# A planner's rule for operations on one PSUM tile: dependence on every earlier operation of the other engines instead of the latest of each, with a new table of due-time offsets

## The chip, the cores and the metric

The kernel runs on one core of one Trainium2 chip. The metric is device time in microseconds, the median of three runs. One execution was also profiled; rows quoted below come from that one.

## What is computed

Pooled attention followed by a feed-forward layer with a rational activation, 4608 tokens (8 x 576), model width 512 (8 heads of 64), hidden width 2048:

```python
k_p = k.reshape(B, H, S // 8, 8, D).mean(axis=3)      # same for v
scores = q @ k_p.T / sqrt(D)
attn = softmax(scores)
x = (attn @ v_p) as (B*S, H*D)
h = x @ w_in
P = a[0] + a[1]*h + a[2]*h*h + a[3]*h*h*h
Q = 1 + abs(b[0])*abs(h) + abs(b[1])*h*h
out = (P / (Q + 1e-6)) @ w_out
```

The weights arrive in 64-bit floats; the kernel decodes each into a high and a low 32-bit part, and splits activations the same way, so that each large product is three products (high x high, low x high, high x low).

## The kernel before

The 4608 tokens are 18 blocks of 256 (`i`), the hidden width is 8 units of 256 (`u`): 144 units (i, u), listed in `order` (lines 942 to 945). For a block, `attend` (line 787) prepares pooled keys and values, makes scores, softmax and the attention output `x` (tiles `qT`, `ps`, `mx`, `e`, `sm`, `am`, `pv`, `x`). For a unit, `mm1` (line 837) makes `ph` = h in a PSUM bank with 24 matmuls on TensorE, `rational` and `quotient` (lines 850 and 866) turn it into `gh` and `gl`, and `mm2` (line 887) adds their products with `wout` into two PSUM banks `po` with 24 matmul halves. After a block's last unit the `po` are evicted and stored.

The quotient of one unit is a chain over three engines. ScalarE (ACT) makes `w` = |h| (line 867), `t` = a3 h + a2 (line 868) and `r` = b1 w + b0 (line 869). GpSimd (POOL) multiplies `w` by `r` (line 870). VectorE (DVE) makes `t` times h (line 871) and then (t + a1) times h (line 872). ACT takes the reciprocal of the denominator as Ln and Exp into the PSUM tile `rp` (lines 874, 875); DVE joins the two sides in three steps (lines 876 to 881); ACT copies the high part `gh` (line 882), POOL makes the low part `gl` (line 883). Lines 867, 868, 871 and 872 all read the PSUM tile `ph`. `w`, `t` and `r` lie in a ring of seven buffers (`rat`, line 381); the operation `w` claims all three tiles of its unit (`claims=early`), the operation `t` only its own.

None of this is issued in the order of the text. Each operation is handed to `Plan.add` (line 146) with an engine, a cost and a due time. `add` collects dependencies: by data, and for tiles in PSUM (`ring.tag == "ps"`, lines 169 to 173) on operations of other engines. Due times come from `due(at)` (line 948) with `HEAD`, `PACE`, `SLOW` (line 946); the second half of a unit is due five units later (`LAG`). `solve` (line 189) carries due times backwards along the dependencies, adds the hand-made or searched offsets of the table `LATER` (by operation number, line 115), and then fills the engines greedily: on each engine the operation that can start first, and among those within 0.02 us of it the one due first (lines 237 to 239). `issue` (line 283) emits the operations in the order found. Each engine then executes its own list strictly in that order, and the framework puts the semaphores: an operation on a PSUM tile waits for what other engines were issued on that tile before it, reads included.

Line 315 issues every planned operation, so every row of the profile carries L315, and groups are told apart by tile names; line 307 issues filler matmuls at the start (`idle`).

Of the kernel before, what the change touches and what calls it, by code (L numbers as in the profile page):

```python
# [22 lines left out]
class Lazy:  # L23


    def __init__(self, tile, chain=()):
        self.tile, self.chain = tile, chain
# [41 lines left out]
def meet(a, b):  # L69
    return all(x0 < y1 and y0 < x1 for (x0, x1), (y0, y1) in zip(a, b))  # L70


class Buf:


    def __init__(self, ring, shape, dtype, name):
        self.ring, self.shape, self.dtype, self.name = ring, shape, dtype, name
        self.writes, self.reads, self.left, self.held, self.it = [], [], 0, False, None
        self.slot, self.latest = None, {}

    def real(self):
        if self.it is None:
# [18 lines left out]
class Plan:  # L101
# [11 lines left out]


    LATER = {
# [15 lines left out]
    }  # L131
    HOLD = {}

# [12 lines left out]
    def add(self, eng, cost, calls, port=False, claims=(), bytes=0, early=34.0, after=()):  # L146
        op = Op()
        op.eng, op.cost, op.port, op.calls, op.bytes = eng, cost, port, calls, bytes
        op.early, op.slack, op.lead = early, self.slack, 0.0
        op.seq, op.due, op.deps, op.users = len(self.ops), self.now, set(), []  # L150
        touched = {}
        for _, args, kw in calls:
            every = list(args) + list(kw.values())
            dst = kw.get("out", args[0] if args else None)
            for v in every:
                if isinstance(v, Lazy) and v is not dst:
                    box = v.box()
                    op.deps.update(o for o, x in v.tile.writes if meet(x, box))
                    v.tile.reads.append((op, box))
                    touched[id(v.tile)] = v.tile  # L160
            if isinstance(dst, Lazy):
                t, box = dst.tile, dst.box()
                op.deps.update(o for o, x in t.writes if meet(x, box))
                op.deps.update(o for o, x in t.reads if meet(x, box))
                if box == ():
                    t.writes, t.reads = [], [r for r in t.reads if r[0] is op]
                t.writes.append((op, box))
                touched[id(t)] = t
        for t in touched.values():
            if t.ring.tag == "ps":  # L170

                op.deps.update(o for e, o in t.latest.items() if e != eng)
                t.latest[eng] = op
        op.deps.update(after)
        op.deps.discard(op)
        for c in claims:
            touched[id(c.tile)] = c.tile
        op.bufs = list(touched.values())
        for b in op.bufs:
            b.left += 1  # L180
        self.ops.append(op)
        return op
# [151 lines left out]
def tile_pooled_attention_then_rational_moe(  # L334
# [32 lines left out]
    NA = NU // 2  # L367
# [575 lines left out]
    order += [(i, u) for u0 in (0, NA) for i in (2, 3) for u in range(u0, u0 + NA)]  # L943
    order += [(i, u) for i in range(2) for u in range(NA, NU)]
    order += [(i, u) for i in range(4, NBLK) for u in range(NU)]
    HEAD, PACE, SLOW, SLOWS = 15.0, 5.5, 4.5, 2 * NA

    def due(at):
        return HEAD + SLOW * min(at, SLOWS) + PACE * max(0, at - SLOWS)
# [78 lines left out]
```

## Time and profile before

| | |
|---|---|
| median of 3 runs | 913.93 us (913.83 to 915.69) |
| the profiled execution | 912.12 us |
| its span | 910.2 us |
| TensorE busy | 887.5 us, 98% |
| VectorE busy | 761.2 us, 84% |
| ScalarE busy | 675.0 us, 74% |
| GpSimd busy | 526.1 us, 58% |

The span is the time from the first to the last instruction of the profiled execution; 1.9 us of that execution lie outside it. PE is TensorE's matmuls, PEld its weight loads, which run ahead of the matmuls. "Idle before" and the brackets at the end of a timeline row say how long the engine had nothing to do before that instruction, and which instruction ended it.

### The profile page before, as it was taken

What the parts mean: (1) busy time and instruction counts of PE and PEld (TensorE: products, weight loads), DVE (VectorE), ACT (ScalarE), POOL (GpSimd) and SP (SyncE); (2) the same over time, 40 slices, a digit from 0 to 9 for tenths busy, and PEclk for the clock granted to TensorE, in tenths of its full rate; (3) what the DMA queues carried; (4) which work ended last, traced back from release to release, by engine and by line L of the source; (5) the groups of instructions that cost most, each with busy time, mean ns of one, the idle gap of its engine ahead of it and who ended that gap; (6) DMA issues with size and microseconds to landing.
All of it is one profiled execution on the core that took longest, in us unless ns stands there. A gap on an engine that the chain in (4) does not pass through costs nothing.

```text
span 910.2 us, 17165 instructions
## 1 busy us (share of the span) xinstructions
PE 887.5 (98%) x6132; PEld 823.3 (90%) x6132; DVE 761.2 (84%) x1337; ACT 675.0 (74%) x1124; POOL 526.1 (58%) x472
## 2 busy tenths in 40 slices
PE   8899999999999999999999999999999999999998
PEld 7898899899998999999999899989888999999997
DVE  7899888879889899959997888798979899578874
ACT  4799879859487868658886675785849697577874
POOL 5776867876357545446745743546635754435554
PEclk9999999999999999999999999999999999999999
DMA  9994201154144312122603341323322411202000
GB/s 294 344 393 150 53 24 47 47 149 96 43 91 115 84 31 57 30 54 60 138 10 72 93 88 35 48 50 99 79 45 59 93 45 31 52 1 35 25 24 23
DMA packets 185081, 75.31 MB, mean 83 GB/s; under 512 B 162341, under 2 KB 162341, under 8 KB 184997
## 3 DMA queue, kind: packets, MB, share of 16 engines
q1 hardware_dynamic: 184996, 74.23, 31.3%
q8 instruction: 48, 0.79, 0.4%
q14 instruction: 37, 0.29, 0.1%
HBM read 50.59 MB, written 12.58 MB: 69 GB/s over the span
## 4 chain that ended last, share of the span: by engine, by line
PE 55%; ACT 18%; DVE 12%; SPq 5%; issue 4%; DMA 4%; POOL 2%; ACTq 0%; POOLq 0%; DVEq 0%
PE ph L315 25%; PE po L315 22%; DVE t L315 6%; SPq L315 5%; ACT rp L315 4%; ACT r L315 3%; ACT t L315 3%; ACT w L315 3%; PE ps L315 3%; PE pv L315 2%; ACT gh L315 2%; DMA q<-in_q_dram 2%; DVE rp L315 1%; ACT am L315 1%; DMA st_v<-in_v_dram 1%
## 5 line engine op out<-in xcount | busy, mean ns | idle before, releaser
L315 PEld LDWEIGHTS ph<-x,win 128*128 128x128 f32 x3264 | 436.4, 191 | 28.1 <-DVE t L315 1.0
L315 PE MATMUL ph<-x,win 128*128 128x256 f32 x3264 | 447.5, 276 | 2.2 <-DVE t L315 0.9
L315 PE MATMUL po<-wout,gh 128*128 128x512 f32 x1152 | 325.6, 383 | 2.6 <-ACT gh L315 1.4
L315 POOL TENSOR_TENSOR w<-w,r 128x512 f32<-128x512 f32 (+1 forms) x145 | 190.9, 1317 | 213.1 <-ACT r L315 197.1
L315 POOL TENSOR_TENSOR gl<-t,gh 128x512 fp32r<-128x512 f32 (+1 forms) x145 | 190.9, 1318 | 92.3 <-ACT gh L315 75.5
L315 PEld LDWEIGHTS po<-wout,gh 128*128 128x128 f32 x1152 | 193.3, 191 | 18.3 <-ACT gh L315 3.2
L315 PE MATMUL po<-wout,gl 128*128 128x512 f32 x576 | 174.1, 384 | 1.3 <-POOL gl L315 1.1
L315 DVE SCALAR_TENSOR_TENSOR t<-t,abn,rp 128x512 f32<-128x512 f32 (+1 forms) x145 | 106.4, 734 | 49.2 <-ACT rp L315 48.4
L315 ACT ACTIVATE w<-ph 128x512 f32<-128x512 f32 (+1 forms) x145 | 85.8, 592 | 68.2 <-PE ph L315 54.0
L315 ACT ACTIVATE rp<-w,cbias 128x512 f32<-128x512 f32 (+1 forms) x145 | 99.7, 687 | 45.6 <-POOL w L315 41.3
L315 DVE TENSOR_TENSOR t<-t,ph 128x512 f32<-128x512 f32 (+1 forms) x145 | 97.9, 676 | 37.9 <-ACT t L315 25.5
L315 ACT ACTIVATE r<-w,abn 128x512 f32<-128x512 f32 (+1 forms) x145 | 117.3, 809 | 1.6 <-POOL w L315 0.4
L315 ACT ACTIVATE t<-ph,abn 128x512 f32<-128x512 f32 (+1 forms) x145 | 111.5, 771 | 5.9 <-PE ph L315 3.8
L315 ACT CAST gh<-t 128x512 fp32r<-128x512 f32 (+1 forms) x145 | 88.5, 612 | 31.9 <-DVE t L315 14.2
L315 DVE SCALAR_TENSOR_TENSOR t<-t,abn,ph 128x512 f32<-128x512 f32 (+1 forms) x145 | 106.6, 736 | 4.7 <-ACT w L315 2.5
L315 PEld LDWEIGHTS po<-wout,gl 128*128 128x128 f32 x576 | 95.6, 191 | 9.1 <-POOL gl L315 3.1
L315 DVE SCALAR_TENSOR_TENSOR t<-rp,t 128x512 f32<-128x512 f32 (+1 forms) x145 | 98.2, 677 | 1.8
L315 DVE SCALAR_TENSOR_TENSOR rp<-w,rp 128x512 f32<-128x512 f32 (+1 forms) x145 | 98.9, 682 | 0.1
L315 ACT ACTIVATE rp<-rp 128x512 f32<-128x512 f32 (+1 forms) x145 | 84.6, 583 | 1.6
L315 POOL TENSOR_TENSOR e<-e,sm 128x576 f32<-128x576 f32 x36 | 42.4, 1191 | 41.7 <-DVE sm L315 19.9
L315 PE MATMUL pv<-am,vm 128*128 128x256 f32 (+3 forms) x288 | 47.9, 282 | 2.1 <-DVE am L315 1.4
L315 PEld LDWEIGHTS pv<-am,vm 128*128 128x128 f32 x288 | 42.7, 192 | 5.0 <-DVE am L315 2.1
(109 smaller groups left out, 849.1 us busy)
## 6 DMA issues: line engine op xcount, KB each, us to landing
am<-e SPq DMA_DIRECT2D x224, 48.0 KB, 2.1
out_dram<-ob SPq DMA_DIRECT2D x17, 512.0 KB, 3.5
rwin<-in_moe_w_in_dram SPq DMA_DIRECT2D x8, 1024.0 KB, 12.7
rwout<-in_moe_w_out_dram SPq DMA_DIRECT2D x8, 1024.0 KB, 14.2
st_k<-in_k_dram SPq DMA_DIRECT2D x12, 512.0 KB, 4.5
st_v<-in_v_dram SPq DMA_DIRECT2D x12, 512.0 KB, 3.9
q<-in_q_dram SPq DMA_DIRECT2D x144, 32.0 KB, 2.0
st_v<-in_v_dram SPq DMA_DIRECT2D x48, 64.0 KB, 2.2
```

What stands on the lines that cost most here:

```text
L315: getattr(engines[op.eng], name)(*map(value, args), **{k: value(v) for k, v in kw.items()})
```

## The change

In `Buf`, the record of the latest operation of each engine becomes a list of all operations on the tile. In `add`, an operation on a PSUM tile depends on every operation of other engines in that list. The table `LATER` is replaced (129 entries by 82), and `PACE` goes from 5.5 to 5.7 us per unit.

```diff
-        self.slot, self.latest = None, {}
+        self.slot, self.users = None, []
...
     LATER = {
-        50: 2, 56: -5, 85: -5, 133: 5, 140: 6, 162: 13, 177: 2, 188: 1.3, 189: -2, 213: 18,
-        224: 0.01, 228: -3, 229: 15, 277: 8, 309: 8, 329: 5, 346: -4, 392: -6, 430: 12, 455: -14.1,
...
-        4920: 12, 4992: 7, 5050: 16, 5061: 17, 5068: 8, 5076: 4.3, 5102: 3.3, 5218: 15, 5232: 14,
-        5265: 10,
+        50: 1.2, 66: 2, 124: -11, 158: 15, 160: 5, 176: 7, 240: 10, 247: 23, 294: 8, 297: -19,
+        340: 9, 346: 6, 416: 6, 445: -18, 576: 7, 582: 3, 606: 6, 626: 8.5, 701: -7, 707: -5,
...
+        4286: -26, 4287: -2, 4384: 5, 4405: 5, 4432: 10, 4456: 11, 4533: 12.6, 4562: 12,
     }
...
             if t.ring.tag == "ps":
 
-                op.deps.update(o for e, o in t.latest.items() if e != eng)
-                t.latest[eng] = op
+                op.deps.update(o for o in t.users if o.eng != eng)
+                t.users.append(op)
...
-    HEAD, PACE, SLOW, SLOWS = 15.0, 5.5, 4.5, 2 * NA
+    HEAD, PACE, SLOW, SLOWS = 15.0, 5.7, 4.5, 2 * NA
```

Of the entries named later: operation 213 is a load of the second block's queries (`q1`), 176 the load of the weight unit `win1`, 445 a load of keys of the second sequence.

## Rows read from the trace of the kernel before

**Rows 1.** The page's first part: busy us (share of the span) xinstructions
```profile
span 910.2 us, 17165 instructions
PE 887.5 (98%) x6132; PEld 823.3 (90%) x6132; DVE 761.2 (84%) x1337; ACT 675.0 (74%) x1124; POOL 526.1 (58%) x472
```

**Rows 2.** Stretches: length, busy us (x) by engine, clock, DMA share, GB/s
```profile
0.00:50.00 50.00, 43.55 (x309) 40.71 (x310) 40.24 (x78) 30.54 (x56) 32.52 (x70) 0.97 1.01 327
50.00:150.00 100.00, 98.90 (x695) 90.45 (x695) 88.48 (x143) 90.95 (x148) 76.76 (x52) 1.00 0.36 123
150.00:292.00 142.00, 138.69 (x956) 127.42 (x955) 121.94 (x211) 106.08 (x175) 91.91 (x76) 1.00 0.36 91
292.00:413.00 121.00, 120.56 (x839) 113.31 (x838) 101.34 (x182) 88.50 (x145) 60.60 (x51) 1.00 0.24 52
679.00:708.00 29.00, 27.73 (x174) 24.98 (x173) 27.15 (x44) 25.80 (x45) 14.95 (x13) 1.00 0.26 60
906.00:910.20 4.20, 0.08 (x1) 0.00 (x0) 0.00 (x0) 0.60 (x1) 0.00 (x0) 1.00 0.33 125
...
150.00:906.00 756.00, 744.97 (x5132) 692.15 (x5130) 632.51 (x1117) 552.88 (x921) 416.81 (x352) 1.00 0.27 61
```

**Rows 3.** Waits of the weight loads, whole span: us in total, times, longest
```profile
PEld po L315 <- ACT gh L315: 3.2, 8, 0.8
PEld po L315 <- POOL gl L315: 3.1, 6, 1.2
PEld pv L315 <- DVE am L315: 3.0, 4, 1.6
```

**Rows 4.** Waits of the matmuls themselves, whole span
```profile
PE pq L315 <- DMA q<-in_q_dram: 2.2, 1, 2.2
...
PE po L315 <- ACT gh L315: 1.4, 5, 0.4
```

**Rows 5.** Waits between ACT and DVE around the PSUM tile ph, whole span
```profile
ACT w L315 <- DVE t L315: 12.9, 24, 1.2
...
DVE t L315 <- ACT w L315: 5.3, 9, 1.0
```

**Rows 6.** Timeline from 698 to 705 us: start, us, instruction [idle before <-releaser]
```profile
698.47 0.75 ACT L315 ACTIVATE t<-ph,abn 128x512 f32<-128x512 f32 x1
...
699.27 0.68 DVE L315 TENSOR_TENSOR t<-t,ph 128x512 f32<-128x512 f32 x1
...
700.46 0.74 DVE L315 SCALAR_TENSOR_TENSOR t<-t,abn,ph 128x512 f32<-128x512 f32 x1
...
701.24 0.60 ACT L315 ACTIVATE w<-ph 128x512 f32<-128x512 f32 x1 [0.30 <-DVE t L315]
...
703.10 0.61 ACT L315 CAST gh<-t 128x512 fp32r<-128x512 f32 x1
...
703.76 0.30 PEld L315 LDWEIGHTS po<-wout,gh 128*128 128x128 f32 x2 [0.81 <-ACT gh L315]
```

**Rows 7.** Timeline: weight loads held at four other places, and w before two
```profile
263.47 0.60 ACT L315 ACTIVATE w<-ph 128x512 f32<-128x512 f32 x1 [0.49 <-DVE t L315]
...
266.00 0.73 PEld L315 LDWEIGHTS po<-wout,gh 128*128 128x128 f32 x4 [0.55 <-ACT gh L315]
...
552.74 0.30 PEld L315 LDWEIGHTS po<-wout,gl 128*128 128x128 f32 x2 [0.71 <-POOL gl L315]
...
586.67 0.73 PEld L315 LDWEIGHTS po<-wout,gh 128*128 128x128 f32 x4 [0.52 <-ACT gh L315]
...
808.41 0.60 ACT L315 ACTIVATE w<-ph 128x512 f32<-128x512 f32 x1 [0.82 <-DVE t L315]
...
812.06 0.73 PEld L315 LDWEIGHTS po<-wout,gh 128*128 128x128 f32 x4 [0.35 <-ACT gh L315]
```

**Rows 8.** Instructions on tile am: duration ns min/median/max, first and last start
```profile
L315 DVE TENSOR_TENSOR am<-am,am x14: 1181/1222/2324, 219.3 to 846.8; 128x1024 fp32r<-128x1024 f32 x14
...
L315 DVE TENSOR_TENSOR am<-am,e x14: 687/690/1804, 223.7 to 849.9; 64x512 fp32r<-64x512 f32 x14
```

17 rows, old and new, of the table LATER are left out of this document.

## The prediction

> **What bounds the kernel now.** I read the busy times first, then TensorE's idle time by stretch, then its waits, then the timeline behind single waits. TensorE is busy 887.5 of 910.2 us [rows 1], and no other engine is above 84%. So the time is TensorE's fixed work plus the moments in which it has nothing to do: the change adds and removes no matmul, and it can move only the 22.7 us of idle time, and only in TensorE's favour or against it. They lie as follows [rows 2]: 6.45 us in the first 50 us, 1.10 us from 50 to 150, 11.03 us from 150 to 906 (756.00 less 744.97), and 4.12 us after the last matmul, while the final tile is evicted and stored.
>
> The waits say who ends the idle time. The weight loads stand first in TensorE's queue and feel a late operand first. For the second product they wait 3.2 us for `gh` in eight pieces and 3.1 us for `gl` in six, and for the attention output 3.0 us for `am` in four [rows 3]. The matmuls' own idle behind `gh` is smaller, 1.4 us [rows 4], because loads run ahead and part of a late load is covered. The losses are some thirty short holds, not one broken stage.
>
> One wait looks odd and belongs to this change. ACT's `w` (|h|) waits 24 times, 12.9 us in all, for a DVE step on `t` [rows 5]. `w` reads only `ph`, so by data it needs nothing but TensorE. The timeline shows the cause [rows 6]: ACT makes `t` at 698.47, DVE then does its two steps that read `ph`, at 699.27 and 700.46, and the unit's `w` starts at 701.24, right where the second ends (701.20). `t` was issued first, the DVE steps before `w`, and so `w`, which also reads the bank, has to wait for them. The planner does not know that wait: in `add` the DVE step depends on the *latest* ACT operation on `ph`, which is `t`, and `w` is left free to fall behind; `w` needs three free ring buffers and `t` one, so when the ring is short `t` goes first. The plan puts `w` where nothing stands in its way on paper, and on the chip everything behind it in ACT's list slips by the wait. (The Trainium skill, "PSUM — Partial Sum Buffer", section "PSUM bank collisions raise a hardware error", says that two engines must not touch one bank at once, reads against reads included, so a semaphore has to order them. The trace agrees: those 24 waits are between two readers [rows 5].)
>
> **The change part by part.**
>
> *The new dependence.* For most PSUM tiles it says nothing new, since the operations are already chained by data or touch the tile from two engines only. It is new for `ph`: the DVE steps of lines 871 and 872 now come after `w` too; and for the eight key preparations, whose short copies I cost at nothing. What it removes: cases as the one just read [rows 6]. There the slip reaches TensorE: `gh` ends at 703.71 and the weight load at 703.76 has waited 0.81 us. The same picture stands at four other places [rows 7], a `w` held for 0.45 to 0.82 us (two of the four stand in the group) and two to six us behind it a load of `po` held: 0.55 us at 266.00, 0.71 us at 552.74 (through `gl`), 0.52 us at 586.67, 0.35 us at 812.06. With the one before, that is 0.55 + 0.71 + 0.52 + 0.81 + 0.35 = 2.94 us. Bounds: 1.4 us if only the matmuls' own idle behind `gh` counts [rows 4], 6.3 us if every hold on `gh` and `gl` came from it [rows 3]. I take 2.9 us, since these five I could follow to a held `w`; the other 19 of the 24 waits ended in slack [rows 5].
>
> *What it adds.* A DVE step that used to run ahead of `w` now waits for it. Nine such waits exist today, 5.3 us, 0.59 us each [rows 5]; 24 more would be 14.2 us. Behind a waiting DVE step stand, in the same list, the softmax steps, `qT`, `am` and the joins of other units, and for those ACT (`gh`) and TensorE (`pv`, `ps`) wait. What hides it: DVE is idle 149 us of the span [rows 1], and the planner now sees the wait and can put other DVE work ahead. I cost it at nothing; without that cover it is the slower rival below.
>
> *Due times anew, and the pace.* For the last unit (number 143) the due time goes from 15 + 36 + 5.5 x 135 = 793.5 to 15 + 36 + 5.7 x 135 = 820.5 us, later by 27. Due times only rank operations that could start together, so this costs nothing by itself, but with 129 offsets taken out and 82 others put in, the order on every engine is dealt again after the first tens of us. The holds that have nothing to do with `w` (about 11.03 less 2) will lie elsewhere and have other sizes. Bounds from the stretches [rows 2]: the quietest long one, 292 to 413, idles 0.44 us of 121 (0.36%), which over 756 us would be 2.7 us, a gain of 8.3 in all; the worst long one, 150 to 292, idles 3.31 of 142 (2.33%), 17.6 us, a loss of 6.6. I see no reason for either end and take zero, so the value lies near the mean of what is there.
>
> *The head.* The loads change rank: a load of `q1` loses an offset of +18 and `win1` gets +7, both in favour of `q1`, for which TensorE waits 2.2 us [rows 4]; the keys' load of operation 445 now gets -18, against it, in a stretch in which the DMA engines are full (share 1.01) [rows 2]. Between a gain and a loss of 2.2 us; I take zero.
>
> *The sum.* 2.9 us less. The profiled execution took 912.12 us, 1.9 us of it outside the span, so its like would be 909.2; the median of the runs is 913.93, 1.81 us above the profiled one, so the median should be 911.0 us.
>
> **The rivals.** *The gain is dealt out again (no change).* The holds behind `am` are not the bank's. The DVE step `am<-am,e` takes 690 ns as a rule and 1804 at worst, `am<-am,am` 1222 and 2324 [rows 8]: single instances run over a microsecond long, and TensorE's 3.0 us on `am` [rows 3] lie behind such. The new dependence does nothing for them, and a new order can lay two or three more of them before a block's `pv`: three at 1.1 us cancel the 2.9. It gives about 913.5 us. (The Trainium skill, "SBUF — State Buffer", section "Who interferes with whom", has a rule that speaks for this rival: a DVE instruction with two SBUF inputs and a GpSimd instruction that reads SBUF exclude each other for the whole instruction. The long `am` steps have two SBUF inputs, and 1804 ns is about one GpSimd step more than 690; by this rule alone the time would stay where it is.) To this outcome also belongs that the order around `w` hardly changes, because it does not do what it says: 24 waits [rows 5] speak against that. 913.9 us.
>
> *DVE is held up (slower).* Place: stretches where DVE has no room, as 679 to 708, busy 27.15 of 29.00 [rows 2]: 1.85 us free, three waits of 0.59. From a fourth `w` in such a stretch on, the waits push `am`, `qT` and the `ph` banks' release back. If half of 14.2 us reaches TensorE, that is 7.1 less 2.9: 4.2 us slower, 918.1 us. For it: DVE is the second busiest engine. Against it: the planner now counts that wait, while it did not count the one on `w`.
>
> *The plan comes out as quiet as 292 to 413 (faster by more).* All unseen holds and the slips that follow from them go: 8.3 us less, 905.6 us. For it: an error of half a microsecond moves three engines against each other, and later holds may be its children. Against it: the long `am` steps.
>
> **How the numbers follow.** Forecast, two to five us less, 911.0: 0.40. Quiet plan, 905.6: 0.14. No change by either way, 913.5: 0.24. DVE held up, 918.1: 0.22. A measurement of this kernel can tell about 0.2% (1.8 us) from no change. Faster: 0.40 + 0.14 = 0.54; same 0.24; slower 0.22. The range from 905.0 to 917.5 takes in the quiet plan and all but the far half of the slower case; the forecast's own range is 909 to 912.
>
> **What would show it.** Right: in the changed kernel `ACT w` hardly ever waits for `DVE t` (from 24 times, 12.9 us, to under 2 us), and in each unit `w` precedes the DVE product; `DVE t` waits for `ACT w` more than nine times; the weight loads' waits on `gh` and `gl` fall from 6.3 us to about 3; TensorE's idle time from 150 to 906 us is near 8 us. Wrong: `w` no longer waits but the idle time in that stretch is still 11 us or more, with longer holds on `am`, `qT` or `ph`; or a wait of more than 2.2 us for a load in the first 50 us.

## The result, and the profile after

The changed kernel takes 900.8 us (median of five runs, 898.9 to 902.0) against 913.9 us before; the ratio is 0.985, with a 95% interval of 0.983 to 0.986. That is 13.1 us less, where 2.9 us less was forecast, and it lies 4.2 us under the lower end of the range. Its profiled execution has a span of 897.2 us.

The first part of the page of the changed kernel, to be read against [rows 1]; its operations carry L309, since the shorter table moves line 315 up:

```profile
span 897.2 us, 17205 instructions
PE 881.1 (98%) x6124; PEld 823.8 (92%) x6124; DVE 753.1 (84%) x1337; ACT 683.2 (76%) x1124; POOL 521.3 (58%) x472
```

The busy time of the matmuls fell by 6.4 us although no matmul of the computation was removed (of the fillers, there are 46 now with 9.2 us busy, and were 54 with 9.3). The busy time of the weight loads stayed (823.3, now 823.8), so it is their idle time that fell: 910.2 - 823.3 = 86.9 us before, 897.2 - 823.8 = 73.4 us now, 13.5 less where the span is 13.0 shorter.

Stretches of the changed kernel (length, busy by engine, clock, DMA), to be read against [rows 2]:

```profile
0.00:50.00 50.00, 42.81 (x288) 39.52 (x289) 36.60 (x76) 31.24 (x58) 33.90 (x71) 0.97 1.00 313
50.00:150.00 100.00, 99.73 (x720) 92.42 (x720) 90.48 (x149) 92.82 (x149) 73.44 (x53) 1.00 0.39 130
...
150.00:893.00 743.00, 738.55 (x5120) 691.81 (x5118) 626.06 (x1114) 558.52 (x918) 413.96 (x350) 1.00 0.27 62
893.00:897.20 4.20, 0.03 (x1) 0.00 (x0) 0.00 (x0) 0.60 (x1) 0.00 (x0) 0.82 0.33 125
```

TensorE's idle time is 7.19 us in the first 50 us (6.45 before), 0.27 us to 150 (1.10), and 4.45 us from there to the last matmul (11.03). By its idle time, the gain lies in the long part from 150 us on, not at the start.

Waits in the changed kernel, in total, times, longest: the one wait left between ACT's `w` and DVE's `t`, then some of the weight loads', then a matmul's at the start. They answer [rows 3, 4, 5]:

```profile
DVE t L309 <- ACT w L309: 5.1, 6, 2.3
```
```profile
PEld pv L309 <- DVE t L309: 4.1, 2, 2.5
...
PEld po L309 <- ACT gh L309: 0.9, 2, 0.6
...
PEld pv L309 <- DVE am L309: 0.6, 2, 0.4
...
PEld po L309 <- POOL gl L309: 0.3, 1, 0.3
```
```profile
PE pq L309 <- DMA q<-in_q_dram: 2.8, 1, 2.8
```

The wait of `w` for `t` (24 times, 12.9 us) is gone. But the loads' waits for `gh`, `gl` and `am` fell together from 9.3 to 1.8 us, also those that no held `w` stood behind. One wait grew, that of the loads of `pv` for a DVE step `t`; before it was

```profile
PEld pv L315 <- DVE t L315: 1.1, 1, 1.1
```

Both loads that wait now, at 270.39 and 506.74 us, start 0.06 us after the end of a unit's last DVE step on the PSUM tile `rp`. So they probably wait for a PSUM bank to come free; no run tests that. For `am` and `t` together, the loads of `pv` wait 4.7 us in the changed kernel and 4.1 before.

What had changed for them shows in the timeline of the changed kernel, for the unit of [rows 6] (block 13, unit 3): its `gh`, and the first weight load that uses it.

```profile
689.56 0.61 ACT L309 CAST gh<-t 128x512 fp32r<-128x512 f32 x1
...
697.36 0.74 PEld L309 LDWEIGHTS po<-wout,gh 128*128 128x128 f32 x4
```

`gh` ends at 690.17, and is used 7.19 us later. In the kernel before it ended at 703.71 and was used at 703.76. So the question for the experiments became what had taken that time to spare in the kernel before: the dependence or the table.

### The profile page after: what moved, and what is told of

Read it like the earlier page. It is cut to its first block, busy times and chain, and to the rows that moved or that the text cites. A ratio compares the mean times of both kernels' runs of the same rounds, so it can differ in the third digit from the quotient of the medians.

```text
span 897.2 us, 17205 instructions
## 1 busy us (share of the span) xinstructions
PE 881.1 (98%) x6124; PEld 823.8 (92%) x6124; DVE 753.1 (84%) x1337; ACT 683.2 (76%) x1124; POOL 521.3 (58%) x472
## 4 chain that ended last, share of the span: by engine, by line
PE 81%; ACT 6%; SPq 4%; DMA 3%; DVE 2%; issue 2%; POOL 1%; POOLq 0%; ACTq 0%; DVEq 0%
PE po L309 36%; PE ph L309 36%; PE pv L309 4%; SPq L309 4%; PE ps L309 3%; DMA early<-in_v_dram 2%; ACT rp L309 1%; DVE t L309 1%; ACT r L309 1%; DVE m_wout L309 1%; ACT w L309 1%; ACT t L309 1%; POOL wout L309 1%; DMA ob<-pd 0%; ACT wout L309 0%
## 5 line engine op out<-in xcount | busy, mean ns | idle before, releaser
L309 PEld LDWEIGHTS ph<-x,win 128*128 128x128 f32 x3264 | 455.1, 191 | 32.0 <-issue 0.7
L309 PE MATMUL ph<-x,win 128*128 128x256 f32 x3264 | 464.7, 276 | 0.5 <-ACT x L309 0.4
L309 PE MATMUL po<-wout,gh 128*128 128x512 f32 x1152 | 333.5, 383 | 0.5 <-POOL wout L309 0.3
L309 POOL TENSOR_TENSOR w<-w,r 128x512 f32<-128x512 f32 (+1 forms) x145 | 188.4, 1300 | 216.7 <-ACT r L309 181.3
L309 POOL TENSOR_TENSOR gl<-t,gh 128x512 fp32r<-128x512 f32 (+1 forms) x145 | 189.4, 1307 | 84.3 <-ACT gh L309 70.1
L309 PEld LDWEIGHTS po<-wout,gh 128*128 128x128 f32 x1152 | 187.3, 191 | 10.6 <-ACT gh L309 0.9
L309 PE MATMUL po<-wout,gl 128*128 128x512 f32 x576 | 172.6, 382 | 0.1
L309 DVE SCALAR_TENSOR_TENSOR t<-t,abn,rp 128x512 f32<-128x512 f32 (+1 forms) x145 | 106.8, 736 | 67.2 <-ACT rp L309 65.6
L309 ACT ACTIVATE rp<-w,cbias 128x512 f32<-128x512 f32 (+1 forms) x145 | 99.7, 687 | 55.0 <-POOL w L309 48.6
L309 ACT ACTIVATE w<-ph 128x512 f32<-128x512 f32 (+1 forms) x145 | 85.9, 592 | 50.3 <-PE ph L309 49.7
L309 ACT ACTIVATE r<-w,abn 128x512 f32<-128x512 f32 (+1 forms) x145 | 117.3, 809 | 3.0 <-DVE rp L309 1.6
L309 ACT ACTIVATE t<-ph,abn 128x512 f32<-128x512 f32 (+1 forms) x145 | 111.7, 772 | 10.2 <-PE ph L309 8.6
L309 DVE TENSOR_TENSOR t<-t,ph 128x512 f32<-128x512 f32 (+1 forms) x145 | 97.7, 675 | 18.8 <-ACT t L309 12.8
L309 DVE SCALAR_TENSOR_TENSOR t<-t,abn,ph 128x512 f32<-128x512 f32 (+1 forms) x145 | 106.4, 734 | 1.8
L309 ACT CAST gh<-t 128x512 fp32r<-128x512 f32 (+1 forms) x145 | 88.7, 613 | 21.2 <-PE po L309 17.9
L309 DVE SCALAR_TENSOR_TENSOR t<-rp,t 128x512 f32<-128x512 f32 (+1 forms) x145 | 98.2, 678 | 1.4
L309 DVE SCALAR_TENSOR_TENSOR rp<-w,rp 128x512 f32<-128x512 f32 (+1 forms) x145 | 98.9, 682 | 0.2
L309 PEld LDWEIGHTS po<-wout,gl 128*128 128x128 f32 x576 | 93.8, 191 | 4.9 <-POOL gl L309 0.3
L309 ACT ACTIVATE rp<-rp 128x512 f32<-128x512 f32 (+1 forms) x145 | 84.3, 581 | 2.4
L309 POOL TENSOR_TENSOR e<-e,sm 128x576 f32<-128x576 f32 x36 | 42.9, 1206 | 30.3 <-DVE sm L309 22.2
L309 PE MATMUL pv<-am,vm 128*128 128x256 f32 (+3 forms) x288 | 47.4, 284 | 3.7 <-DVE t L309 3.7
L309 PEld LDWEIGHTS pv<-am,vm 128*128 128x128 f32 x288 | 42.4, 194 | 4.3 <-DVE t L309 4.1
## 6 DMA issues: line engine op xcount, KB each, us to landing
rwout<-in_moe_w_out_dram SPq DMA_DIRECT2D x8, 1024.0 KB, 12.9
```

The lines of the kernel that those rows point to most:

```text
L309: getattr(engines[op.eng], name)(*map(value, args), **{k: value(v) for k, v in kw.items()})
```

## The experiments

Four theories are named in the expectations. A: the gain is the holds of `w` that the planner did not see. B: it is the new table and pace. C: the old table's entries for blocks 4 to 17 make operands arrive just in time, so that every small delay reaches TensorE. D: it is the first 300 us. "Early" entries are those below operation 1385, the first matmul of block 4's first unit; "late" ones the rest. The old table has 42 early and 87 late entries (two expectations say 91, a miscount), the new one 36 and 46. The line number in a profile row changes with the length of the table.

Two things were counted for each kernel in its own trace. The second product has 12 matmuls of 512 columns for each unit (1728 in the trace), so the end of the 384th marks the end of 32 units (blocks 0 to 3), and the last the end of 144. And for each `gh` and `gl` of blocks 4 to 17 (224 tiles), the time from its end to the first weight load that uses it: the time to spare. "Held" are the units whose `w` is issued behind their first DVE product. In the table, "old" and "new" are those of the two kernels, and "own" is a table of the run's own. Its last three columns come from one profiled execution of each kernel, which lies up to 3.0 us under the median (h1) or 2.4 us over it (new_none_57).

| kernel | dependence | pace | early | late | held | median us | to unit 32 | units 33 to 144 | spare under 1 us |
|---|---|---|---|---|---|---|---|---|---|
| before | old | 5.5 | old | old | 43 | 913.9 | 249.7 | 656.4 | 50 |
| i1_before_pace57 | old | 5.7 | old | old | 39 | 918.3 | 256.7 | 655.8 | 35 |
| f2_before_tail_table | old | 5.5 | none | old | 39 | 911.0 | 251.0 | 654.1 | 51 |
| h1_old_rule_old_late | old | 5.7 | new | old | 39 | 907.5 | 245.8 | 652.6 | 34 |
| g1_after_old_late | new | 5.7 | new | old | 0 | 907.3 | 248.6 | 653.0 | 30 |
| e1_rule_alone | new | 5.5 | old | old | 0 | 915.4 | 257.1 | 651.5 | 30 |
| after | new | 5.7 | new | new | 0 | 900.8 | 247.2 | 645.8 | 13 |
| e2_table_alone | old | 5.7 | new | new | 25 | 902.1 | 249.1 | 644.9 | 17 |
| f1_before_head_table | old | 5.5 | old | none | 9 | 903.3 | 252.4 | 644.6 | 1 |
| f3_after_head_table | new | 5.7 | new | none | 0 | 900.9 | 251.7 | 644.9 | 1 |
| new_none_57 | new | 5.7 | none | none | 0 | 906.1 | 257.4 | 644.8 | 1 |
| g3_old_none_55 | old | 5.5 | none | none | 4 | 902.2 | 252.8 | 643.2 | 1 |
| old_none_57 | old | 5.7 | none | none | 2 | 898.8 | 251.3 | 641.9 | 1 |
| h2_slack_kept | new | 5.71 | own | own | 0 | 898.7 | 247.6 | 643.5 | 1 |

The planner also reckons an end of its own plan (the latest `done` in `solve`, when that kernel's plan is solved): 886.3 us for the kernel before, 886.3 without the late entries (f1), 890.4 without any entry (g3), 893.6 for e1, 887.2 for old_none_57 and 885.1 for the changed kernel. So on paper the late entries change nothing and the old table is worth 4.1 us at its pace; what follows is what they do on the chip.

**The dependence alone** (e1): the change in `add` and `Buf`, with table and pace as before.

```diff
-                op.deps.update(o for e, o in t.latest.items() if e != eng)
-                t.latest[eng] = op
+                op.deps.update(o for o in t.users if o.eng != eng)
+                t.users.append(op)
```

> The new dependence alone: table of offsets and pace as before. Theory A (holds the planner did not see): before, 43 units issue w behind the DVE product of the same unit; here none does, so most of the 13.1 us goes even though the table was made for the other order: 902 to 908 us, and ACT w hardly waits for DVE t. Theory B (the new table and pace pay): nothing is won without them, 912 us or more.

Measured 915.4 us, ratio 1.0025 (1.0015 to 1.0036): no gain, though no unit is held any more. Theory A falls in its simple form. But the two parts of the kernel differ: from unit 33 on it is 4.9 us faster than before (651.5 against 656.4), and up to unit 32 it is 7.4 us slower (257.1 against 249.7). The plan itself is 7.3 us longer here (893.6 against 886.3), presumably because the old table was made for the other dependence.

**Table and pace alone** (e2): the kernel before with the new `LATER` and

```diff
-    HEAD, PACE, SLOW, SLOWS = 15.0, 5.5, 4.5, 2 * NA
+    HEAD, PACE, SLOW, SLOWS = 15.0, 5.7, 4.5, 2 * NA
```

> The new table of offsets and the new pace with the old dependence. In its issue order 25 units have w behind the DVE product again. Theory A: 25 of 43 holds, 25/43 of 13.1 us = 7.6 us slower than the changed kernel, 906 to 910 us. Theory B: the table and the pace do the work, 900 to 903 us, like the changed kernel.

Measured 902.1 us, ratio 0.988 (0.987 to 0.990), as theory B has it. In 25 units `w` is behind again, and that costs TensorE little. The waits of `w` in this kernel, and of the loads on `gh`:

```profile
ACT w L309 <- DVE t L309: 6.4, 11, 1.5
```
```profile
PEld po L309 <- ACT gh L309: 1.4, 3, 0.8
```

Eleven holds of 6.4 us together, and 1.3 us between this kernel and the changed one (902.1 against 900.8), while the runs of each scatter by 2.5 to 3.1 us.

**No table at all**, with either dependence at pace 5.7, and the old one at 5.5. The edit is

```diff
     LATER = {
-        50: 2, 56: -5, 85: -5, 133: 5, 140: 6, 162: 13, 177: 2, 188: 1.3, 189: -2, 213: 18,
...
     }
```

> Old dependence, no table at all, pace 5.7. Only 2 units have w behind the DVE product. Theory A: the old table was what put w behind, so without it the old dependence is nearly harmless: 902 to 908 us, well under before. Theory B: a table is what makes the time, so without one it is at or above before, 914 to 920 us.

Measured 898.8 us, ratio 0.984 (0.983 to 0.986). The old dependence without any offset is 15 us faster than with its table. That is faster than any theory had it (A said 902 to 908). Theory B falls too, in the form that a table makes the time: the old one costs.

> New dependence, no table, pace 5.7. Theory A: no w behind the DVE product, so within 2 us of the old dependence without a table (902 to 908 us); the rest to 900.8 is what the new table is worth. Theory B: 914 to 920 us without a table.

Measured 906.1 us, ratio 0.993 (0.992 to 0.995). That is in theory A's range, but 7.4 us slower than the old dependence, where A allowed 2. The two profiled executions differ by 9.2 us; 6.1 of these are lost before unit 33 (257.4 against 251.3), of which 2.6 show as idle time of TensorE in the first 50 us (8.52 against 5.95 us).

> Old dependence, no table, pace 5.5; at pace 5.7 this took 898.8 us. If the pace is a part of the gain by itself: 902 to 906 us. If it only ranks: 897 to 901 us. 4 units have w behind the DVE product.

Measured 902.2 us, ratio 0.987 (0.986 to 0.989): without a table, the pace of 5.7 is worth 3.5 us.

**Early and late entries apart.** The kernel before with early entries only (f1), with late entries only (f2), the changed kernel with early entries only (f3). The edit of f1:

```diff
-        1038: 18, 1307: 7, 1415: 10, 1435: -14, 1442: 8, 1460: 2, 1535: -14, 1606: 10, 1653: -15,
...
-        5265: 10,
+        1038: 18, 1307: 7,
```

> The kernel before (old dependence, pace 5.5) with only the entries of its table below operation 1385, the first of block 4; the 91 entries for blocks 4 to 17 are left out. Theory C (the late entries make operands arrive just in time, so that each small delay on the chip reaches TensorE): TensorE's idle time after 300 us nearly goes, 900 to 905 us. Theory A (holds of w): only 9 units have w behind the DVE product instead of 43, so 902 to 906 us as well. Theory D (the first 300 us, where the new table differs too, make the gain): within 2 us of before, 912 to 916 us.

Measured 903.3 us, ratio 0.989 (0.987 to 0.991). Leaving out nothing but late entries gives back 10.5 us. By itself this does not part theory C from A, which forecast 902 to 906 us, since the held units also fall from 43 to 9; g1 and h1 below do. The stretch from 300 us to its last matmul:

```profile
300.00:897.40 597.40, 594.56 (x4138) 558.45 (x4136) 499.93 (x887) 444.27 (x739) 317.22 (x272) 1.00 0.25 55
```

2.84 us of idle time there. The kernel before, over the same stretch:

```profile
300.00:906.00 606.00, 598.28 (x4123) 557.23 (x4121) 502.62 (x889) 440.00 (x735) 318.52 (x270) 1.00 0.24 53
```

7.72 us. And no `gh` or `gl` is used within half a microsecond of its end, where 36 of 224 were.

> The complement: the kernel before with only the 91 entries from operation 1385 on. Theories C and A: the bad stretch after 300 us stays, and the untuned head costs a few us more: 913 to 920 us. Theory D: the head without entries as in the old dependence without a table (898.8 at pace 5.7): 898 to 904 us.

Measured 911.0 us, ratio 0.997 (0.996 to 0.998), below the lower end that A and C gave, but far from the 898 to 904 of D: the late part is as slow as before (654.1 us).

> The changed kernel with only the entries of its table below operation 1385; its entries for blocks 4 to 17 are left out. Theory C: the late entries buy nothing and take slack, so 897 to 901 us, the same or 1 to 3 us faster than the changed kernel (900.8). Against C: the late entries of the new table are worth something, 903 us or more.

Measured 900.9 us, ratio 0.986 (0.983 to 0.989), the same as the changed kernel: the new late entries neither help nor harm beyond what runs scatter.

**Delays put in.** ACT's `w` is issued twice, one behind the other, in 24 units, without the planner's knowledge, which adds 0.59 us each, 14 us in all. They are the units in which `w` waits in the kernel before; other units were not tried, so the choice may weigh against that kernel:

```diff
-            for name, args, kw in op.calls:
+            calls = op.calls
+            if op.eng == "act" and isinstance(calls[0][1][0], Lazy) and (
+                    calls[0][1][0].tile.name in self.TWICE):
+                calls = calls * 2
+            for name, args, kw in calls:
```

> The changed kernel, with the ACT operation w issued twice, one behind the other, in 24 units, those in which w waited for DVE t in the kernel before: 24 delays of about 0.5 us in ACT that the plan did not count. It leaves nothing out. Theory A (each unseen delay of ACT costs the end): 24 x 0.5 us = 12 us, 909 to 914 us. Theory C (slack takes them): 901 to 904 us.

> The kernel before with the ACT operation w issued twice in the same 24 units as in the run with 24 slips of the changed kernel; it leaves nothing out. There the slips cost 3.3 us (904.1 against 900.8). Theory C (before has no time to spare): clearly more, 920 to 926 us. If delays cost the same in both kernels: 916 to 918 us.

> The kernel before without its late entries (903.3 us), with ACT's w issued twice in the same 24 units; it leaves nothing out. The same slips cost 12.7 us in the kernel before (926.4) and 3.3 us in the changed one (904.1). If the late entries are what takes the time to spare: 3 to 5 us, 906 to 909 us. If the spare time lies elsewhere (dependence, pace, early entries): 10 to 13 us, 913 to 916 us.

The same 24 delays cost 3.3 us in the changed kernel (904.1), 12.7 us in the kernel before (926.4, ratio 1.013, 1.012 to 1.015), and 7.3 us in the kernel before without late entries (910.7 against 903.3). The waits of the loads for `gh` in the kernel before with the delays, then in the changed kernel with them:

```profile
PEld po L320 <- ACT gh L320: 10.1, 15, 1.7
PEld po L320 <- POOL gl L320: 4.6, 8, 1.2
```
```profile
PEld po L314 <- ACT gh L314: 3.6, 4, 1.5
```

In the kernel before, the waits on `gh` grow from 3.2 [rows 3] to 10.1 us: there was little to take the delays up. The third run is a partial miss, between its two ranges. Its waits on `gh` are small (1.5 us, three times), but it still loses 7.3 us. In the profiled executions the first 32 units grew by 3.9 us in the kernel before, 2.4 without late entries and 3.2 in the changed kernel, about the same in all three; units 33 to 144 grew by 10.4, 4.8 and 0.9. So there the late entries are somewhat more than half of the difference in sensitivity (10.4 less 4.8, of 10.4 less 0.9), and the rest lies in something that `gh` does not show.

**The late entries against the dependence.** The changed kernel with the old late entries (g1), and the same with the old dependence (h1).

```diff
-        1024: -1, 1032: 9, 1134: 1, 1194: 5, 1221: 21, 1252: 7, 1329: -4, 1589: 15, 1605: 3.4,
+        1024: -1, 1032: 9, 1134: 1, 1194: 5, 1221: 21, 1252: 7, 1329: -4, 1415: 10, 1435: -14,
...
```

> The changed kernel (new dependence, pace 5.7, its own entries below operation 1385), but with the old table's entries for blocks 4 to 17 in place of its own. No unit has w behind the DVE product. Theory A (holds of w are what the old late entries cost): 899 to 903 us, as the changed kernel. Theory C (the old late entries leave operands no time to spare, whatever the dependence): 909 to 912 us. Half of each: 904 to 908 us.

> As the run with the changed kernel's early entries, pace 5.7 and the old late entries (907.3 us), but with the old dependence; 39 units have w behind the DVE product, there none. This isolates the dependence where the late entries are the old ones. If the holds of w are the other half of the gain: 912 to 915 us. If the dependence is worth nothing and the rest came from the head or the pace: 906 to 909 us.

Measured 907.3 us (ratio 0.992, 0.991 to 0.994) and 907.5 us (0.993, 0.991 to 0.995). The first lies in the range that was set for half of A and half of C, the second where the dependence is worth nothing. The old late entries cost 6.5 us with the new dependence and no hold at all, and 5.4 us with the old one (907.5 against 902.1); the dependence between the two is worth 0.2 us, less than the runs of h1 scatter (904.4 to 911.3). In h1 the loads wait longer for `gh`, 4.6 us, than in g1, 2.2 us, although the profiled execution of h1 (904.4) is shorter than that of g1 (907.6); what made up for it is not shown.

```profile
ACT w L299 <- DVE t L299: 10.5, 17, 1.7
...
PEld po L299 <- ACT gh L299: 4.6, 7, 1.4
```
```profile
PEld po L314 <- ACT gh L314: 2.2, 4, 1.1
```

**The pace alone** (i1): the kernel before with 5.7 for 5.5.

> The kernel before with the pace alone changed, 5.7 for 5.5. With old dependence, old late entries, pace 5.7 and the new early entries the time was 907.5. If the pace makes the difference between that and before: 907 to 910 us. If the early entries make it: 912 to 917 us.

Measured 918.3 us, ratio 1.006 (1.004 to 1.008): 5.2 us slower than before in the same comparison (913.1), and 1.3 us over the upper of the two ranges. The pace helps where no table was made for another one, and harms the old early entries (256.7 us to unit 32, 249.7 before). With the new early entries and pace 5.7 the same late entries give 907.5 (h1).

This makes a chain from the kernel before to the changed one, one part at a time: the pace 5.2 us slower (i1), the early entries 10.8 faster (h1), the late entries 5.4 faster (e2), the dependence 1.3 faster. The parts depend on each other: in f1 the late entries alone gave 10.5. Up to unit 32 the pace and the early entries go against each other (7.0 more, 10.9 less). From unit 33 on, leaving out or replacing the old late entries wins 11.8 us in f1, 7.7 from h1 to e2 and 7.2 from g1 to the changed kernel.

**A version made for time to spare** (h2): the new dependence, 43 entries, none after operation 1570.

```diff
-    HEAD, PACE, SLOW, SLOWS = 15.0, 5.7, 4.5, 2 * NA
+    HEAD, PACE, SLOW, SLOWS = 14.9, 5.71, 4.42, 2 * NA
```

> A version made on the finding: new dependence, no entries beyond operation 1570, 43 entries in all, chosen among plans of the same planned length as the changed kernel's for how little small random delays of ACT, DVE, POOL and DMA lengthen them; HEAD 14.9, PACE 5.71, SLOW 4.42. If time to spare is what was missing: 895 to 899 us, under the changed kernel (900.8) and the old dependence without a table (898.8). If that is exhausted: 899 to 903 us.

Measured 898.7 us (897.0 to 899.6), ratio 0.983 (0.981 to 0.985). Its median is 2 us under the changed kernel's, and level with the old dependence without a table (898.8). The intervals of the three ratios overlap, so a lead over the changed kernel is not shown; but the simplest version, the old planner with an empty table at pace 5.7, is no slower than it in these runs.

## Why the prediction was wrong, point by point

*TensorE as the bound: right. Its 887.5 us of busy time as fixed work: wrong.* The matmuls of the same computation were busy for 881.1 us after the change. The records of single matmuls overlap, so busy time is not their sum. This is the largest group, before and after:

```profile
L315 PE MATMUL ph<-x,win 128*128 128x256 f32 x3264 | 447.5, 276 | 2.2 <-DVE t L315 0.9
```
```profile
L309 PE MATMUL ph<-x,win 128*128 128x256 f32 x3264 | 464.7, 276 | 0.5 <-ACT x L309 0.4
```

3264 matmuls of 276 ns would be 901 us, and their busy time is half of that. (A group's own busy time also depends on how its matmuls are mixed with others, so it can rise while the total falls.) A short wait between two such matmuls need not leave a gap, so the idle time, 22.7 us, was not all that there was to win. Of the 13.0 us of span, 6.4 came out of the busy time and 6.6 out of the idle time; that the 6.4 were such hidden waits is likely, but not shown. (The Trainium skill, "Trainium Kernel Development and Optimization", section "Performance Expectations", warns that matmul busy time is a bad measure of how close a kernel is to its roofline, because matmuls are pipelined, and names the weight loads' busy share as one of two good ones. These two traces agree: the loads' busy time is the same to 0.5 us, and their idle time fell by 13.5.)

*The holds of `w`, 2.9 us: the sign in the trace was right, the worth was not.* The wait of `ACT w` for `DVE t` disappeared, as forecast, and the loads' waits on `gh` and `gl` fell from 6.3 to 1.2 us, further than the 3 that were forecast. But the dependence by itself gave 2.2 us more (e1, 915.4 against 913.2 of before in the same comparison), 0.2 less (g1 against h1), 1.3 less (the changed kernel against e2) and 7.4 more (no table). Only in e1 from unit 33 on did it win clearly, 4.9 us. The five stalls that I followed back [rows 6, 7] did have a held `w` ahead of them, but the hold was only the last push: each of these `gh` and `gl` was ready 0.05 us before its load started, and in the changed kernel the same five tiles were ready 4.0 to 9.7 us ahead of theirs. A hold of half a microsecond costs little there, as the eleven holds of e2 show.

*The added wait of DVE at nothing: right.* `DVE t` waited for `ACT w` six times, 5.1 us, against nine and 5.3 [rows 5]; I had said more than nine. The slower rival built on it did not come.

*Due times anew at zero: this is the step that failed.* I took the redealt order as having no sign, and set the ends from two stretches' idle time, a gain of 8.3 to a loss of 6.6 us. It was nearly the whole gain: e2 has the redealing without the dependence and takes 902.1 us, 11.1 less than before in the same comparison. Of the 13.0 us of span, 10.6 lie in units 33 to 144 (656.4 to 645.8) and 2.5 before. All six kernels with the old late entries need 651.5 to 656.4 us there, all eight without them 641.9 to 645.8, whichever dependence, pace and early entries they have. Leaving them out and nothing else wins 10.5 us. So there was a sign to be had from the trace of before, if I had looked at it: how long before its use each `gh` and `gl` is ready. 50 of 224 came within a microsecond, and of the thirteen other schedules in the table twelve have fewer. I read who ended each wait, and not how close all the others were. The count parts the two groups of kernels, but does not rank those within a group: i1 has 35 such tiles and e1 30, and i1 is 4.3 us slower there.

*The quiet plan, 905.6 at 0.14: nearest to what happened, but too small and too unlikely.* The holds behind `am` and `qT` shrank with the rest, as would be expected from delays that spare time covers. Its size came from idle time alone, which fell by 6.6 us where this rival had 8.3, and so missed the 6.4 us that came out of the busy time.

*The rival with the long `am` steps:* they are still there, tile `am` in the changed kernel, to be read against [rows 8]:

```profile
L309 DVE TENSOR_TENSOR am<-am,am x14: 1217/1226/1706, 221.6 to 822.7; 128x1024 fp32r<-128x1024 f32 x14
...
L309 DVE TENSOR_TENSOR am<-am,e x14: 687/690/1675, 224.8 to 825.9; 64x512 fp32r<-64x512 f32 x14
```

A single `am<-am,e` still takes 1675 ns, but TensorE's loads now wait 0.6 us for `am` instead of 3.0. With the wait for `t` shown above, the loads of `pv` wait about as long as before (4.7 and 4.1 us), so this rival was right that they keep waiting, though no longer mostly for `am`, and wrong that this would cancel the gain. By the rule of the Trainium skill that I set beside it the time would have stayed. The step of 1675 ns, from 688.21 us, runs beside a GpSimd step from 687.06 us that took 2.27 us, which agrees with the rule; that the time stays does not follow from it.

*The head at zero: about right.* There is 0.74 us more idle time in the first 50 us and 0.83 less from 50 to 150. The wait for the second block's queries is 2.8 us instead of 2.2; I had named more than 2.2 as a sign of being wrong, but it decided nothing.

**What stays open.** That the redealt order makes the gain, and the old late entries the loss from unit 33 on, is shown by the runs. That these entries cost time because they leave `gh` and `gl` no time to spare is argued from the counts and from the delays, which agree with it in part. It is not shown why the delays put in cost 7.3 us in the kernel before without late entries and 3.3 us in the changed kernel, although the first has fewer `gh` and `gl` without time to spare (1 tile under 1 us against 13). Pace and early entries differ between the two, and neither was tried with delays by itself. Nor is it shown why the new dependence without a table loses 6.1 us before unit 33, or how the early entries and the pace act there.

## What to carry to other kernels

When a planner's order has been adjusted with a list of offsets, leave its parts out one by one on the chip: here 87 of 129 offsets could go for a gain of 10.5 us, although the planner's own reckoning put them at nothing. In a trace, beside who ended each wait, count how early operands are ready before the bounding engine uses them. Where many were just in time, 24 small delays of ScalarE, 14 us together, cost 12.7 us, and removing one kind of delay won nothing by itself. And compare two orders by the idle time of the weight loads rather than by the matmuls' busy time, but only where the number of loads is the same: e1 has 58 more loads than the kernel before, all of them fillers that the planner puts into gaps, and by their idle time (80.6 us against 86.9) it would look faster, which it is not.

## What the runs showed of the hardware that was not expected

TensorE's busy time differed by 6.4 us between two orders of the same computation, with the same 5184 matmuls in its two large products. The granted clock does not explain it: it was 1.00 in all stretches from 50 us to the last matmul in the kernel before, and 0.99 or 1.00 in the changed one, which is the faster. And two engines that only read one PSUM tile wait for each other in the order of issue, by the semaphores that the framework puts: ScalarE waited 12.9 us for VectorE so before and not at all after, VectorE 5.3 us for ScalarE before and 5.1 after. Removing the 12.9 us by itself (e1) did not shorten the whole.
